# M2 of the large blocks as products of 12-bit parts, with the units of weights' parts and the fourth block's first steps at other places

## The chip, the cores and the metric

The kernel runs on one core of a Trainium2 chip. The engines work side by side, each on its own queue in program order: TensorE (PE; PEld is its weight load), VectorE (DVE), ScalarE (ACT), GpSimd (POOL), and SyncE (SP), which here issues the DMAs. The metric is the device time of one execution in microseconds (us). All times inside the kernel are counted from the start of its span.

## The reference

A retention layer for 4 x 8 heads over 768 positions of width 64, whose output, as 3072 tokens x 512, goes through a layer with ELU:

```python
for t in range(S):
    state = gamma[None, :, None, None] * state + np.einsum('bhd,bhe->bhde', k[:, :, t], v[:, :, t])
    y[:, :, t] = scale * np.einsum('bhd,bhde->bhe', q[:, :, t], state)
...
h = x @ w_in
g = np.where(h > 0.0, h, alpha * (np.exp(np.minimum(h, 0.0)) - 1.0))
return (g @ w_out).astype(np.float32)
```

`w_in` is 512 x 2048 and `w_out` 2048 x 512, all in float32.

## The kernel before

**Token blocks.** The 3072 tokens are six blocks of 512 (tb 0 to 5). Blocks 0 and 1 go through the two layers by themselves; blocks 2 and 3, and then 4 and 5, go together as "large blocks" (nb 0 and 1 in the loop `for nb in range(NB)`). Retention is done in chunks of 128 tokens (`scores`, `states`, `outputs`: 64 x 64 products), and each step of it is set by hand between the products of the layers: `retention_step(tb, step)`.

**Products.** The layers use a seven-product scheme (products 1 to 7, or M1 to M7 for a large block). A float32 matmul of TensorE is two records in the trace. In a large block's first layer, M2, M1, M3 and M7 are each split again into seven products (`big_twice`, products at L1268, two calls with `at` 0 and 1 for each M; `ORDER1`), and so M2 too is done "by two levels". M6 and M4 are done another way (`passes`, L1330): weights and inputs are cut into parts of 12 bits, so that a product of two parts is exact in one pass over the rows. With `hi` and `lo` parts of the weights, and a third plane that serves the correction (`d`), a 128-row tile takes six matmuls of 512 columns: four with `hi` and `lo`, two with `d`. The results are put together by `stt(..., 4097.0, ...)`, which is one VectorE instruction. M5 is plain float32 (`big_rest`, L1317). Then `second_big` (L1376) is the second layer. For blocks 0 and 1 the first layer of block 1 is `first` / `strassen` (L784) and the second layer `second_twice` (L977).

**Parts of weights.** A unit (n, j) is a quarter of layer j's weights. `parts_of_layer` (L919) takes a tile, makes `hi` on ScalarE (L923), `lo` on VectorE (L917) and `d` on GpSimd (L925), and gives back two sends of 512 KB and 256 KB, which go to DRAM (`scratch5`). The sends are issued by SyncE in program order and wait there for the tile's VectorE and GpSimd instructions. `next_part` (L1701) issues the sends of the unit before and begins the next one. The list `units` has eight; six are made during the first layer of block 1 (rounds n = 0 to 3 of the loop at L1706: two in round 1, three in round 2, one in round 3), in two tiles of the pool `wide`, and two in `side` of the first large block, in the tile of the pool `x6`. A tile is written again when both sends of the unit that had it have landed.

**A round.** In a round, products 1 and 2 of round n are issued, between them and after them products 3 and 4 of round n - 1, and then 6, 7 and 5. ScalarE copies results out of the PSUM banks: `kept` (L726, after products 6 and 5), and `nc.scalar.copy(pb, pa)` (L743), which must be done before product 2 adds onto bank pb. Places in a round at which a unit can be begun: after product 2, then `at` 0, 1 and 2, after products 6, 7 and 5. In round 3, retention of block 2 starts: four masks (L342), four scalings of v on VectorE (`scale_v`, L305).

**Weights from DRAM.** After round 3 the ring of slots opens: eight tiles of 256 KB and, while block 1's second layer runs, three more. `want(...)` lists the pieces in the order of their use; `fetch` (L854) issues a load whenever a slot is free, and `done` gives a slot back behind the product that read it. All loads of weights, the chunks of q, k, v (1 MB each, `load`, L125), the sends (`send_small`, L679) and the stores of the output share SyncE's queue. In the first large block, products 1, 2 and 4 of `big_twice` read their weights from `w_all`, so that M2 loads 1 MB; in the second one, 1.75 MB. The sums of M2's weights are made by `combine_small(2)` and sent beside the first layer of block 1, and `send_quarters(2)` sends the rest. `big_x(j)` makes M_j's inputs, four VectorE subtractions; `split_x` (L933) makes the three planes of an input to `passes`, one ScalarE and two VectorE instructions.

## Time and profile before

| | |
|---|---|
| median of 3 runs | 615.33 us (614.37 to 616.35) |
| the profiled execution | 612.33 us |
| its span, first to last instruction | 610.6 us |

Busy us of the engines by stage, and the mean busy share of the 16 DMA engines:

| stage (us) | what | PE | DVE | ACT | POOL | DMA share | GB/s |
|---|---|---|---|---|---|---|---|
| 133 to 183 | first layer of block 1, parts | 49.82 | 43.64 | 25.44 | 8.42 | 0.87 | 279 |
| 183 to 237 | second layer of block 1, retention | 54.00 | 47.05 | 11.07 | 3.49 | 0.91 | 318 |
| 237 to 262 | M2 of the first large block, retention of block 3 | 23.98 | 18.36 | 6.59 | 1.04 | 0.66 | 216 |
| 262 to 298 | its M1, M3, M7 | 36.00 | 33.25 | 22.43 | 3.54 | 0.95 | 293 |
| 298 to 333 | its M6, M4, M5 | 34.79 | 32.84 | 28.98 | 34.15 | 0.84 | 274 |
| 333 to 440 | its second layer, retention of blocks 4 and 5 | 107.00 | 86.61 | 17.58 | 5.60 | 0.58 | 177 |

The stages go on in the same way for the second large block. In a line of the timeline the first number is the start, the second the length of what was merged into the line; in brackets stands the idle time ahead of it and what ended it. Lengths of TensorE's lines overlap, since matmuls are pipelined; the starts tell how long something took. The chain of waits follows the end of the kernel back to what released each step.

### The profile page before, as it was taken

The numbers are of one execution on the slowest core, as the hardware profiler recorded it, in microseconds if no ns is written. First come the engines' busy times: TensorE is split into PE (matmuls) and PEld (weight loads), VectorE is DVE, ScalarE is ACT, GpSimd is POOL, SyncE is SP. The second block draws the span as 40 slices with busy tenths as digits, with TensorE's granted clock in tenths as the row PEclk, the third lists the DMA queues.
The fourth block names the chain that finished last, engine by engine and source line by source line (L and its number), as shares of the span: only waits on it lengthen the run. The fifth ranks groups of instructions, "written<-read, shape, count | busy, mean of one in ns | idle before, by whom it ended". The sixth has DMA issues, their size and how long they took to land.

```text
span 610.6 us, 13767 instructions
## 1 busy us (share of the span) xinstructions
PE 602.7 (99%) x5510; PEld 492.5 (81%) x5510; DVE 506.5 (83%) x778; ACT 262.3 (43%) x448; POOL 97.0 (16%) x75
## 2 busy tenths in 40 slices
PE   8999999999999999999999999999999999999997
PEld 6765568888889998888766888888888866788886
DVE  5769889989799886889998787898658999778785
ACT  6899744205553112147689310100236778611110
POOL 2011000000220001000697000110000398000000
PEclk9999999999999999999999999999999999999999
DMA  8698569789977999599986455874554676656553
GB/s 318 272 389 308 172 215 270 234 244 259 353 236 242 296 394 325 182 299 258 307 286 222 125 136 156 271 272 115 191 166 154 172 206 191 166 152 188 152 151 116
DMA packets 87856, 139.85 MB, mean 229 GB/s; under 512 B 7024, under 2 KB 48752, under 8 KB 83056
## 3 DMA queue, kind: packets, MB, share of 16 engines
q1 hardware_dynamic: 87792, 138.96, 71.3%
q8 instruction: 44, 0.72, 0.5%
q14 instruction: 20, 0.16, 0.1%
HBM read 105.12 MB, written 33.82 MB: 228 GB/s over the span
## 4 chain that ended last, share of the span: by engine, by line
PE 92%; DMA 3%; DVE 2%; POOL 1%; issue 0%; ACT 0%; ACTq 0%; DVEq 0%
PE pa L1376 16%; PE pa L1268 8%; PE pd L1376 8%; PE pa L977 4%; PE pb L1376 4%; PE pd L1268 4%; PE pa L557 3%; PE x L647 3%; PE pa L784 3%; PE x L1330 3%; PE pa L647 2%; PE pa L1317 2%; PE pb L1268 2%; PE sc L331 2%; PE pd L977 2%; PE kv L371 2%
## 5 line engine op out<-in xcount | busy, mean ns | idle before, releaser
L1384 ACT COPY ms<-pa 128x256 f32<-128x256 f32 x41 | 15.2, 372 | 107.5 <-PE pa L1376 103.0
L1376 PE MATMUL pa<-gC,wq 128*128 128x256 f32 x240 | 56.8, 382 | 0.0
L1376 PEld LDWEIGHTS pa<-gC,wq 128*128 128x128 f32 x240 | 45.1, 190 | 7.2 <-issue 1.0
L305 POOL TENSOR_TENSOR chunk<-chunk,vf 128x512 f32<-128x512 f32 x15 | 19.1, 1278 | 164.9 <-DMA chunk<-in_qkv_dram 120.2
L1343 ACT ACTIVATE r<-r 128x512 f32<-128x512 f32 x64 | 40.4, 631 | 2.0
L1279 ACT COPY m<-pa 128x512 f32<-128x512 f32 x32 | 18.7, 584 | 38.5 <-PE pa L1268 35.1
L1388 DVE TENSOR_TENSOR res<-pd,ms 128x256 f32<-128x256 f32 x26 | 11.0, 422 | 28.2 <-PE pd L1376 17.4
L1376 PE MATMUL pd<-w_all,wq 128*128 128x256 f32 x120 | 28.3, 379 | 0.0
L1344 DVE SCALAR_TENSOR_TENSOR gC<-r,gC 128x512 f32<-128x512 f32 x24 | 27.6, 1158 | 0.0
L925 POOL TENSOR_TENSOR wp<-wp 128x512 fp32r<-128x512 f32 x6 | 8.4, 1404 | 116.3 <-DMA scratch_dram<-wi 102.8
L1376 PEld LDWEIGHTS pd<-w_all,wq 128*128 128x128 f32 x120 | 22.8, 190 | 3.1
L1833 POOL TENSOR_TENSOR chunk<-chunk,w_all 128x512 f32<-128x512 f32 x4 | 5.1, 1298 | 127.1 <-DVE gC L1348 127.1
L183 ACT ACTIVATE w_all<-wraw 128x1024 uint32<-128x1024 uint32 (+1 forms) x19 | 19.1, 1007 | 14.0 <-PE x L647 9.8
L1358 DVE TENSOR_TENSOR gC<-w_all,gC 128x1024 f32<-128x1024 f32 x20 | 24.2, 1260 | 0.0
L1376 PE MATMUL pa<-ts,wq 128*128 128x256 f32 x96 | 22.9, 381 | 0.0
L1376 PE MATMUL pa<-w_all,wq 128*128 128x256 f32 x96 | 22.9, 381 | 0.0
L185 ACT ACTIVATE w_all<-wraw 128x1024 fp8e4<-128x1024 f32 (+1 forms) x19 | 22.6, 1190 | 0.6
L1376 PE MATMUL pd<-ts,wq 128*128 128x256 f32 x96 | 22.7, 379 | 0.0
L557 PE MATMUL pa<-xb,w_all 128*128 128x512 f32 x48 | 21.5, 597 | 0.0
L1410 ACT COPY res<-pa 128x256 f32<-128x256 f32 x13 | 4.8, 372 | 38.1 <-PE pa L1376 38.1
L213 DVE CUSTOM_DVE_ANT_0 w_all<-wraw,w_all 128x2048 uint16<-128x2048 uint16 (+1 forms) x19 | 20.1, 1057 | 0.8
L514 ACT ACTIVATE r<-r 128x512 f32<-128x512 f32 x32 | 20.2, 630 | 1.0
(361 smaller groups left out, 1606.7 us busy)
## 6 DMA issues: line engine op xcount, KB each, us to landing
wq<-scratch_dram SPq DMA_DIRECT2D x231, 256.0 KB, 3.5
chunk<-in_qkv_dram SPq DMA_DIRECT2D x22, 1024.0 KB, 7.3
wraw<-in_w_dram SPq DMA_DIRECT2D x15, 1024.0 KB, 6.1
scratch_dram<-wp SPq DMA_DIRECT2D x8, 512.0 KB, 4.0
out_dram<-res SPq DMA_DIRECT2D x7, 512.0 KB, 3.4
scratch_dram<-gT SPq DMA_DIRECT2D x12, 256.0 KB, 4.3
wq<-scratch_dram SPq DMA_DIRECT2D x24, 128.0 KB, 3.2
scratch_dram<-w_all SPq DMA_DIRECT2D x24, 128.0 KB, 3.0
```

The costliest lines, as they stand in the source:

```text
L183: nc.scalar.activation(flat, lo, AF.Copy, scale=2.0**-29)
L185: nc.scalar.activation(top, hi.bitcast(FP32), AF.Copy, scale=2.0**-120, saturate=False)
L213: vec.tensor_tensor(out=flat, in0=c, in1=flat, op=ALU.add)
L514: nc.scalar.activation(e, e, AF.Exp, scale=-1.0)
L557: nc.tensor.matmul(hp, lhsT=w[n][:, fi, j // 2, j % 2, :], rhs=xb[:, j, :], start=(j == 0), stop=(j == 3))
L647: nc.tensor.matmul(X[j][:, d, :], lhsT=w[j][:, d * P : d * P + P], rhs=x[j], start=(n == 0 and d == 0), stop=at_end, skip_group_check=True,)
L977: nc.tensor.matmul(ps, lhsT=w[:, f, :], rhs=ts[j][k][:, f, :], start=(begin and f == 0), stop=(f == 3), skip_group_check=True,)
L1268: nc.tensor.matmul(ps[:, f, :], lhsT=w[:, f, :], rhs=big_xs[j][k], start=(begin and f == 0), stop=True, skip_group_check=True,)
L1343: nc.scalar.activation(r, r, AF.Exp, scale=-1.0)
L1344: return lambda: nc.vector.scalar_tensor_tensor(g, r, -1.0, h, ALU.add, ALU.max)
L1358: nc.vector.tensor_tensor(out=quarter(to, r, t), in0=quarter(x, r, t), in1=quarter(y, r, t), op=op)
L1376: nc.tensor.matmul(ps, lhsT=w[:, f, :], rhs=ts[j][k][:, f // 2, f % 2, :], start=(begin and f == 0), stop=(f == 3), skip_group_check=True,)
```

## The change

- M2 of a large block is done by `one_layer`: for each of eight tiles four matmuls with `hi` and `lo` and two with `d`, one ScalarE copy and one VectorE `stt`. Its input is split by `split_x` into planes: `hi` and `lo` in the tile of `x6`, the third in the pool `top`. `combine_small(2)`, `send_quarters(2)` and `big_x(2)` go.
- Layer 2 joins `LAYER`, and its four units join the list, which now has twelve. They go to `scratch6`, and M2 wants twelve pieces of 256 KB from there.
- The first unit is made in round 0, in a tile of the pool `stage`; three follow in round 1 (after products 2, 7 and 5), four in round 2 (after 2, 6, 7 and 5), two in round 3 (after 2 and 7), all of these in the two `wide` tiles. The last two are made in `side`, at places (2, 2) and (3, 2), where before they stood at (0, 2) and (1, 2).
- `scores(3, 0)` is issued at the end of step 4 of block 1's second layer, and `states(3, 0)` at the end of step 5; the later steps of block 3's retention come a place sooner in the first large block, but for its last, which comes at `at` 2.

```diff
-    W_IN = {1: w_a_[:, :, :, 0], 2: w_a_[:, :, :, 1], 3: w_x_[:, :, :, 1], 7: w_x_[:, :, :, 0]}
-    AMONG = {2: 0, 3: 1, 7: 2, 1: 3}
+    W_IN = {1: w_a_[:, :, :, 0], 3: w_x_[:, :, :, 1], 7: w_x_[:, :, :, 0]}
+    AMONG = {3: 0, 7: 1, 1: 2}
...
-    LAYER = {4: w_b_[:, :, :, 1], 5: w_b_[:, :, :, 0], 6: w_y_}
+    LAYER = {2: w_a_[:, :, :, 1], 4: w_b_[:, :, :, 1], 5: w_b_[:, :, :, 0], 6: w_y_}
...
-        to = scratch5[2 * n : 2 * n + 2].rearrange("f q p c -> q p f c")
-        c = 0 if j == 6 else TH
+        if j == 2:
+            to = scratch6[2 * n : 2 * n + 2].rearrange("f p c -> p f c")
+            third = scratch6[2 * NQ + n].rearrange("p (f c) -> p f c", f=2)
...
     def open_x():
...
+        t = shared["x6"].tile([P, 2, 2, TB], F32R, name="xr", tag="x")
+        return t, open_top([P, 2, 2, TB], F32R)[:, 0]
...
+        for m, i in (("K", 0), ("D", 0), ("K", 1), ("D", 1), ("K", 2), ("K", 3), ("D", 2), ("K", 4), ("K", 5), ("D", 3), ("K", 6), ("K", 7)):
+            want((tb, m, i), scratch6[i + (2 * NQ if m == "D" else 0)])
+        for j, at in ORDER1[2:]:
...
+    def one_layer(n, at):
+
+        tb, banks = n + 2, {}
+
+        def product(m, third):
+            name = (tb, "D", m // 2) if third else (tb, "K", m)
+            ps = bank("bd"[m % 2] if third else "a")
+            todo = [(planes[2][2], m % 2 * TH)] if third else [(planes[2][0], 0), (planes[2][1], TH)]
+            for x, c in todo:
+                for k in range(2):
+                    nc.tensor.matmul(
+                        joined(ps), lhsT=where[name][:, c + k * P : c + k * P + P].bitcast(F32R), rhs=x[:, k],
+                        start=(k == 0 and x is todo[0][0]), stop=(k == 1), skip_group_check=True,
+                    )
+            banks[m, third] = ps
+            if m % 2 or not third:
+                done(name)
+
+        for m in range(4 * at, 4 * at + 4):
+            for third in (True, False) if m else (False, True):
+                product(m, third)
+            if m % 4 == 0:
+                yield
+            nc.scalar.copy(tile_of("C11", m), banks[m, True])
+            stt(tile_of("C11", m), banks[m, False], 4097.0, tile_of("C11", m), ALU.add)
+            if m % 4 in (1, 2):
+                yield
...
-    units, made = [(0, 6), (0, 4), (1, 6), (1, 4), (2, 6), (3, 6), (2, 4), (3, 4)], []
-
-    def next_part(make=True):
+    units, made = [], []
+    units += [(0, 2), (1, 2), (0, 6), (0, 4), (1, 6), (2, 2), (1, 4), (2, 6), (3, 2), (3, 6), (2, 4), (3, 4)]
+
+    def next_part(make=True, pool=None):
         to_send.extend(made)
         send_small()
-        made[:] = parts_of_layer(wide.tile([P, 2, 3, TH], F32R, name="wp", tag="wp"), *units.pop(0)) if make else []
+        made.clear()
+        if make:
+            t = (pool or wide).tile([P, 2, 3, TH], F32R, name="wp", tag="stage" if pool else "wp")
+            made[:] = parts_of_layer(t, *units.pop(0))
...
-        if n > 1:
+        if n:
             next_part()
...
-            if n and at:
-                next_part(n < 3)
+            if n == 2 or n and at:
+                next_part(n < 3 or at < 2)
             if at == 1 and n == 0:
-                some(smalls[2], 2)
+                next_part(True, stage)
...
     def next_block():
-        open_x()
-        run(big_x(2))
+        t, d = open_x()
+        planes[2] = [t[:, 0], t[:, 1], d]
+        split[:] = [split_x(planes[2], xa[:, 2:4])]
+        some(split[0], 2)
...
+        if at == (4, "end"):
+            scores(3, 0)
+        elif at == (5, "end"):
+            states(3, 0)
         if s == ORDER2[-1]:
             break
-    scores(3, 0)
+    run(split[0])
...
-            if units and (at, place) in ((0, 2), (1, 2)):
+            if units and (at, place) in ((2, 2), (3, 2)):
...
-            1: lambda: (send_quarters(2), send_layer(5, range(NQ))), 2: lambda: send_quarters(3),
+            1: lambda: send_layer(5, range(NQ)), 2: lambda: send_quarters(3),
...
-            cur = big_twice(nb, j, sub)
+            cur = one_layer(nb, sub) if j == 2 else big_twice(nb, j, sub)
+            if at == 1:
+                run(tail)
             next(cur)
+            if at == 2:
+                open_quarters()
...
+            if at == 2 and nb == 0:
+                retention_step(3, 4)
...
-            if at == 1 and nb == 0:
-                retention_step(3, 2)
...
             if nb == 0:
                 if at == 0:
-                    states(3, 0)
+                    scores(3, 1)
                 elif at == 1:
-                    retention_step(3, 3)
+                    retention_step(3, 2)
...
                 if at == 0:
-                    scores(3, 1)
                     states(3, 1)
                 elif at == 1:
-                    retention_step(3, 4)
-                    run(tail)
+                    retention_step(3, 3)
```

## The prediction

> **What bounds the kernel now.** I read the page first, then TensorE's timeline around M2, then the queues of ScalarE and SyncE where the parts of weights are made.
>
> ```profile
> PE 602.7 (99%) x5510; PEld 492.5 (81%) x5510; DVE 506.5 (83%) x778; ACT 262.3 (43%) x448; POOL 97.0 (16%) x75
> ```
>
> TensorE is busy 602.7 of 610.6 us at the full granted clock. Time is won only by giving it less to do, and whatever makes it wait is paid in full. The two kinds of product (timeline of TensorE: start, length, line):
>
> ```profile
> 310.95 0.63 PE L1330 MATMUL x<-xl,wq 128*128 128x512 f32 x2
> 311.42 1.09 PE L1330 MATMUL pa<-xr,wq 128*128 128x512 f32 x4
> 312.35 1.88 PE L1317 MATMUL pa<-xb,w_all 128*128 128x512 f32 x4
> ...
> 445.19 1.03 PE L1268 MATMUL pa<-xt,wq 128*128 128x256 f32 x4
> ...
> 451.31 1.03 PE L1268 MATMUL pa<-xt,wq 128*128 128x256 f32 x4
> ```
>
> Lengths overlap, so starts count. Six products of parts (L1330) go from 310.95 to 312.35: 0.233 us each. One half of an M by two levels (L1268; seven rows, 445.19 to 451.31) is 6.12 us.
>
> Where parts are made, ScalarE's timeline shows a wait that TensorE feels:
>
> ```profile
> 163.76 0.57 ACT L726 COPY m<-pa 128x512 f32<-128x512 f32 x1
> 167.13 0.63 ACT L923 ACTIVATE wp<-w_all 128x512 fp32r<-128x512 f32 x1 [2.80 <-DMA scratch_dram<-wp]
> 167.67 0.57 ACT L726 COPY m<-pa 128x512 f32<-128x512 f32 x1
> 169.09 0.63 ACT L923 ACTIVATE wp<-w_all 128x512 fp32r<-128x512 f32 x1 [0.86 <-DMA scratch_dram<-wp]
> 169.63 0.58 ACT L743 COPY pb<-pa 128x512 f32<-128x512 f32 x1
> ```
>
> There are two `wide` tiles, so a unit cannot begin until the store of the unit two before it has landed. Behind it in ScalarE's queue stand the copies that free TensorE's banks. TensorE just got by:
>
> ```profile
> 168.29 1.99 PE L784 MATMUL pa<-xt,w_all 128*128 128x256 f32 x8 [0.18 <-ACT m L726]
> 170.26 1.99 PE L784 MATMUL pb<-xt,w_all 128*128 128x256 f32 x8
> ...
> 183.33 1.16 PE L977 MATMUL pa<-gC,wq 128*128 128x128 f32 x8
> ```
>
> SyncE's queue explains the wait (an entry spans several issues, with the waits between them):
>
> ```profile
> 156.13 0.94 SPq L125 DMA_DIRECT2D chunk<-in_qkv_dram  x2
> 157.16 19.55 SPq L679 DMA_DIRECT2D scratch_dram<-wp  x10
> 176.76 20.59 SPq L854 DMA_DIRECT2D wq<-scratch_dram  x20
> ```
>
> Two loads of 1 MB go ahead of a unit's store, and the chain of waits gives that store this line:
>
> ```profile
> 157.94 9.08 DMA scratch_dram<-wp
> ```
>
> **M2 itself: -2.2 us.** Per block two halves of 6.12 (12.24) become 8 tiles x 6 products x 0.233 = 11.18: -1.06, twice -2.1; I write -2.2 with the switches of shape between halves. Bounds: 0 (rival 4) to -3.2 (with the 1.0 us that TensorE idled at 244 and 249, between the retention products that move). Per tile ScalarE copies once (0.58) and VectorE adds once (0.70), under 1.40 us of TensorE; if that cover went, a bank would be late by the excess alone.
>
> **A. Ten units instead of six in the first layer of the second 512 tokens: +3.4 us.** Unit 1 has a tile of its own; units 2 to 10 share two. Round 1 now makes units 2, 3, 4 and round 2 makes 5, 6, 7, 8. Unit 4 stands where the second unit stood (ScalarE at 154.73, GpSimd done at 157.9); its store still follows the two loads, so it lands at 167.0, and unit 6 starts at 167.1, as in the row. A unit begun there had GpSimd's part done at 169.85, and its 256 KB store took 2.5 us: 172.4. Only then can unit 8 begin, which stands just ahead of the copy to pb; before, that place was reached at 169.09. From there to TensorE's next product took 1.17 us (170.26 - 169.09): 172.45 + 1.17 = 173.6, 3.4 late. Unit 7's wait (store of unit 5, 163.3 + 5.7 = 169.0, then the copy, so L784 at 170.3 for 168.29) lies inside it. Bounds: +0.4 with 2.5 us for unit 4's store too; +6.6 if unit 4 lands 1 us later (more is queued) and unit 6 takes the 4.7 us that the next store took. The first end needs an empty DMA queue, but the DMA share is 0.9 to 1.08 from 148 to 168; I keep the row's value.
> [...]
>
> **B. The ring's first load is late: +3.7 us.** Before, the last sends of parts were through at 176.7 and SyncE went on to the second layer's weights (L854), the first of which took 4.1 us: at hand at 180.9, needed at 183.33. Unit 10 is now made one step later, behind product 7 of round 3. On TensorE's own clock, shifts aside: VectorE is full from 177.39 with four masks (2.41), then this line, of which the first of four stands ahead of the unit:
>
> ```profile
> 179.79 2.48 DVE L305 TENSOR_TENSOR chunk<-chunk,vf 128x512 f32<-128x512 f32 x4
> ```
>
> So unit 10's VectorE part ends at 180.4 + 0.7 = 181.1 and GpSimd's (1.28) at 182.4. Its sends hold SyncE until then, and all ring loads stand behind them: first issue 182.9, landed 187.0, needed at 183.33. Bounds: 1.7 (shortest landing of such a load, 2.1) to 6.2 (6.6, as loads issued at 183 took). Later pieces are no longer late: two further steps of 1.73 us lie between the second and third.
>
> **C. M2's weights in the third block's turn: +1.8 us.** Before, three of seven products read `w_all`, and M2 loaded 1 MB; now 12 pieces of 256 KB, one per 0.93 us, right after a stage in which the DMA is full:
>
> ```profile
> 233.67 0.45 SPq L125 DMA_DIRECT2D chunk<-in_qkv_dram  x1
> 234.22 0.40 SPq L854 DMA_DIRECT2D wq<-scratch_dram  x1
> ...
> 238.41 4.70 SPq L854 DMA_DIRECT2D wq<-scratch_dram  x5
> ```
>
> The piece issued at 234.22 took 8.3 us, to 242.5. In the new order it is the third (K1), wanted 1.9 us after M2 starts at about 236: 4.5 us of waiting at the worst. Against this, the scores and states that move into steps 4 and 5 load no weights and drain about 1 us of backlog, and between 250 and 256 the DMA was idle. Bounds 0 to +4.5; between far ends I take 1.8, nearer the low one, since retention products and the 8 slots can stretch over it. In the fourth turn the DMA share before M2 is 0.51 and the pieces come early: 0.
>
> **The rest: 0.** `scores(3, 0)` and `states(3, 0)` issue no DMA; their chunks were loaded at 197.7 and 209.6 and scaled on GpSimd well before the step, and SyncE is not held by them. They cost TensorE about 1 us each at either place. VectorE loses four subtractions of 0.68 and gains four of 0.69. `split_x` costs ScalarE 1.06 and VectorE 2 x 1.22, for 4 x 0.42 gone; it starts some 4 us ahead of M2, and uncovered it is 0.8 a block. Units 11 and 12 move two M's on (2.8 us of VectorE, where it works 33.25 of 36 us): 0 to +1.5. The waits of their sends hold the ring's loads as they did before, two M's earlier.
>
> Sum: -2.2 + 3.4 + 3.7 + 1.8 = **+6.7 us**; profiled execution 612.33 (span 610.6) to 619.0. The shown median is 615.33, 3.0 above that execution: **622.0**.
>
> **Rivals.** 0.3% (1.85 us) is about what this kernel's measurement tells from no change.
> 1. *The stores land as in an empty queue (other side: not slower).* The eight 128 KB sends of M2's sums leave round 1, which speaks for it; that three units take their place, against. Then A is 0.4, B 1.7, C 0: -2.2 + 2.1 = -0.1, 615.2; if the idle 1.0 and the step before pb are won too, 613. It decides when unit 4's store lands before 163.8, where unit 6 could start. Chance 0.19, 0.11 of it under 613.5. [...]
> 2. *Only one of A and B shows.* The late ring hides behind something that I missed, or A does: +3, 618.3. For it: 1.73 us steps of cover nearby. Against: both waits stand in in-order queues. 0.17.
> 3. *DMA-bound through.* The 2.1 MB of added traffic keeps every landing at 8 us: A 6.6, B 6.2, C 4.5, late units 1, less 2.2: +16, 631. Against: the share falls to 0.38 at 168. 0.08.
> 4. *Products of parts are no cheaper*: at 12.24 / 48 = 0.255 us the gain is gone: 624. The rows show 0.233; 0.03.
> My forecast has 0.53, its own range 618 to 626.
>
> Faster: 0.11. Same: 0.08 of rival 1 and 0.02 of rival 2: 0.10. Slower 0.79. The range 614 to 628 leaves out most of the 0.11 and of rival 3.
>
> **What would show it.** M2's tiles at 1.40 us each (gain). A: L923 waiting some 3 us for `scratch_dram<-wp` three times in round 2, the last ahead of L743, and TensorE idle before pb's L784. B: the first L854 issue about 6 us nearer to the first L977, which waits for `wq`. C: idle of TensorE at the new parts' line on DMA. I am wrong if L923's waits are under 1 us, or if the first L977 follows on without idle time.

## The result, and the profile after

The changed kernel takes 640.61 us (median of 4 runs, 639.33 to 643.36), the kernel before, run beside it, 614.85 us (613.14 to 616.35): 1.0426 times as long, with a 95% interval of 1.0382 to 1.047. The profiled execution took 639.33 us, its span is 637.4 us, 26.8 us more than before. The forecast was 622.0 us: slower was right, the size was not, and neither was the range.

Of the page of the changed kernel, the busy times, TensorE's clock and the chain of waits by engine:

```profile
PE 608.5 (95%) x5494; PEld 492.4 (77%) x5494; DVE 513.7 (81%) x778; ACT 265.9 (42%) x454; POOL 102.4 (16%) x79
...
PEclk9999999999999999897999999999999999999999
...
PE 80%; DMA 8%; DVE 6%; POOL 2%; issue 2%; ACT 1%; SPq 0%; ACTq 0%; DVEq 0%; POOLq 0%
```

TensorE has less to do (16 instructions fewer) and shows 5.8 us more of busy time. Both cannot come from the work, so some of it ran slowly: PEclk, nines all through before, has an 8 and a 7 here, near 255 and 290 us. The mean granted clock is 0.989 where it was 1.000; 0.011 of 637.4 us is 7.0 us. Some 0.9 of it fell into idle time (1.7 us of idle time at half clock between 292.63 and 296.43), where a low clock costs nothing. So about 6 us is an estimate of what the clock alone took. The rest is idle time, and the chain, 92% TensorE before, is 80% now.

Where TensorE waited (its list of waits: what it was about to write and the line, what ended the wait, then us in total, times, the longest):

```profile
PE pa L1276 <- ACT m L1287: 5.5, 1, 5.5
PE pa L1327 <- DMA wq<-scratch_dram: 3.5, 1, 3.5
PE pb L785 <- ACT pb L744: 3.0, 2, 1.7
PE pa L980 <- DMA wq<-scratch_dram: 2.6, 3, 1.8
PE pb L1327 <- DVE xr L916: 2.2, 1, 2.2
```

These five make 16.8 us, two shorter ones for VectorE (1.3 at L1276, 1.0 at L372) another 2.3, and no wait of before is among them. L785 is the first layer, L980 the second layer of block 1, L1327 the new M2 (`one_layer`), L1276 the products of M1, M3 and M7. The largest, 5.5 us, is in a place to which the prediction's sum had given nothing.

Stage lengths in us, by the starts of the same products in each trace. "First layer" runs from its first product on to product 2 of round 3 (the one that waits for the copy to pb), "to layer 2" from there to the first product of block 1's second layer; "layer 2" is cut at the third product behind that one. "M2" ends at M1's second product, "M1, M3, M7" at the first product of M6, and "M2 to M7" is the stretch from M2's first product to M6's first in the second large block (the expectations call it "M2 of the second large block", but M1, M3 and M7 are in it). The last column is the clock of the profiled execution:

| kernel | first layer | to layer 2 | layer 2 | M2 | M1, M3, M7 | M2 to M7, second large block | span | clock |
|---|---|---|---|---|---|---|---|---|
| before | 36.9 | 13.1 | 1.9 + 51.7 | 23.0 | 35.2 | 51.6 | 610.6 | 1.000 |
| changed | 41.3 | 16.2 | 3.5 + 55.7 | 25.3 | 44.9 | 53.6 | 637.4 | 0.989 |
| e1_x6 | 42.5 | 17.0 | 3.6 + 54.5 | 22.4 | 37.4 | 55.5 | 632.2 | 0.992 |
| e7_before_x6 | 37.2 | 13.1 | 1.9 + 52.6 | 23.5 | 49.0 | 51.9 | 628.6 | 0.989 |
| e2_five | 36.4 | 17.3 | 3.6 + 55.3 | 26.4 | 45.1 | 55.8 | 639.8 | 0.979 |
| e5_ring | 36.4 | 16.1 | 1.9 + 54.0 | 26.4 | 44.8 | 55.6 | 636.3 | 0.988 |
| e4_load | 41.5 | 16.1 | 4.4 + 54.7 | 21.6 | 46.5 | 55.6 | 638.1 | 0.984 |
| e3_third | 41.4 | 16.0 | 4.5 + 55.1 | 26.3 | 45.3 | 51.8 | 637.2 | 0.980 |
| e8_fill | 41.8 | 16.2 | 4.3 + 56.9 | 23.6 | 45.7 | 55.6 | 642.1 | 0.984 |
| e9_three | 36.4 | 13.9 | 1.9 + 55.1 | 26.4 | 43.1 | 51.7 | 625.4 | 0.992 |
| e11_four | 37.6 | 13.0 | 1.9 + 54.1 | 22.6 | 37.6 | 51.5 | 615.1 | 1.000 |
| e12_pool | 37.6 | 13.0 | 1.9 + 56.8 | 20.5 | 38.1 | 51.1 | 616.5 | 1.000 |
| e13_split | 37.6 | 13.0 | 1.9 + 55.3 | 20.8 | 39.4 | 51.1 | 616.6 | 0.999 |
| e14_late | 37.6 | 13.0 | 1.9 + 56.8 | 20.1 | 37.3 | 52.0 | 615.7 | 1.000 |

With the change 1.1 us of `states(3, 0)` go from M2's stage to the second layer's. The stages that are not shown differ by at most 2 us. In the changed kernel the stages shown lost 4.3, 3.2, 5.6, 2.4, 9.7 and 2.1 us; the first layer began 0.6 us sooner. The ratios below leave out executions more than 1.5% above the fastest of the same kernel: two of e2's, one each of e11's and e12's.

Three places on ScalarE's queue of the changed kernel (start, length, line; the idle time ahead and what ended it):

```profile
157.23 0.63 ACT L922 ACTIVATE wp<-w_all 128x512 fp32r<-128x512 f32 x1 [2.87 <-DMA scratch_dram<-wp]
...
172.87 0.63 ACT L922 ACTIVATE wp<-w_all 128x512 fp32r<-128x512 f32 x1 [2.63 <-POOL wp L924]
173.41 0.58 ACT L744 COPY pb<-pa 128x512 f32<-128x512 f32 x1
...
292.23 0.63 ACT L922 ACTIVATE wp<-w_all 128x512 fp32r<-128x512 f32 x1 [7.23 <-DMA scratch_dram<-wp]
292.76 0.57 ACT L1287 COPY m<-pa 128x512 f32<-128x512 f32 x1
```

The second and third lines are what the prediction called A: unit 8's step, late, and behind it the copy to pb at 173.41 that TensorE waits for (before: 169.63). Unit 8 needs unit 6's tile, whose `d` was done at 170.27. The idle time is put down to GpSimd's step of unit 7, which ended at 172.77; the chain of waits names the store of unit 6's `d`, which ended at the same moment:

```profile
170.30 2.46 DMA scratch_dram<-wp
```

The first line is one more wait of the same kind, which the prediction did not have: unit 4 waits for unit 2's store, ahead of the copy to pb of round 2, and TensorE stood 1.21 us there. The last pair is the same thing again at a place where nobody had looked. Unit 12 can be written into the one tile of `x6` only when unit 11's store has landed; ScalarE stood 7.23 us, and behind it stood the lift of a bank. SyncE's queue says why the store was late (an entry spans several issues):

```profile
158.61 28.36 SPq L680 DMA_DIRECT2D scratch_dram<-wp  x14
187.02 18.86 SPq L855 DMA_DIRECT2D wq<-scratch_dram  x20
...
279.06 5.28 SPq L680 DMA_DIRECT2D scratch_dram<-wi  x8
284.38 3.13 SPq L680 DMA_DIRECT2D scratch_dram<-w_all  x6
287.61 0.43 SPq L855 DMA_DIRECT2D wq<-scratch_dram  x1
288.14 0.91 SPq L680 DMA_DIRECT2D scratch_dram<-wp  x2
```

VectorE had unit 11 ready at 280.7 (in the large blocks it makes `d` too). Its two sends come last in a queue of fourteen other sends and a load, and are issued at 288.14; the data lands at 292.1. The first two lines are B: the sends of parts hold the queue until 187.0 (before: 176.8), and the second layer's first load with them. In the chain of waits, unit 10's `d` is done on GpSimd at 186.59 and that load, issued at 187.02, lands at 190.23.

TensorE's own queue in the large blocks:

```profile
254.97 1.94 PE L1327 MATMUL pa<-xr,wq 128*128 128x512 f32 x4 [3.50 <-DMA wq<-scratch_dram]
256.84 1.89 PE L332 MATMUL sc<-chunk 64*64 64x64 f32 x64
...
259.23 1.09 PE L1327 MATMUL pa<-xr,wq 128*128 128x512 f32 x4
...
293.38 2.07 PE L1276 MATMUL pa<-xr,wq 128*128 128x256 f32 x4 [5.47 <-ACT m L1287]
296.43 2.07 PE L1276 MATMUL pd<-xr,wq 128*128 128x256 f32 x4 [0.98 <-DVE chunk L1291]
...
469.92 0.62 PE L1327 MATMUL pb<-xr,wq 128*128 128x512 f32 x2
...
471.29 0.61 PE L1327 MATMUL pd<-xr,wq 128*128 128x512 f32 x2
```

Two things are to be read here. The last two rows, one M2 tile apart, start 1.37 us one after the other, the next tile at 472.64 after 1.35, those before after 1.46 and 1.39: the forecast was 1.40. So the work itself became cheaper, by about 1 us a block. And four matmuls that take 1.09 us at 259.23 take 1.94 us right behind the wait of 3.50. The windows of the same kernel give the granted clock there (us; busy time and instructions of PE, PEld, DVE, ACT and POOL; clock; DMA share; GB/s):

```profile
255.00:257.00 2.00, 2.00 (x8) 1.16 (x12) 0.00 (x0) 0.00 (x0) 0.00 (x0) 0.52 0.85 271
...
259.00:261.00 2.00, 2.00 (x54) 1.50 (x56) 1.65 (x3) 0.59 (x1) 0.00 (x0) 1.00 0.89 306
```

Half clock behind a wait, then full clock again; from 293 to 299 us it is 0.50. Of the 9.7 us that M1, M3 and M7 lost, 5.47 + 0.98 are idle time; of the 3.25 left over, some 2.5 are these slow rows, by the starts of the same rows in e1, and 0.29 is a third idle time.

### The profile page after: what moved, and what is told of

Same layout as the page of the kernel before. It is cut to its first block, busy times and chain, and to the rows that moved or that the text cites. A ratio compares the mean times of both kernels' runs of the same rounds, so it can differ in the third digit from the quotient of the medians.

```text
span 637.4 us, 13780 instructions
## 1 busy us (share of the span) xinstructions
PE 608.5 (95%) x5494; PEld 492.4 (77%) x5494; DVE 513.7 (81%) x778; ACT 265.9 (42%) x454; POOL 102.4 (16%) x79
## 2 busy tenths in 40 slices
DMA packets 88687, 144.55 MB, mean 227 GB/s; under 512 B 7088, under 2 KB 46512, under 8 KB 83888
## 4 chain that ended last, share of the span: by engine, by line
PE 80%; DMA 8%; DVE 6%; POOL 2%; issue 2%; ACT 1%; SPq 0%; ACTq 0%; DVEq 0%; POOLq 0%
PE pa L1412 15%; PE pd L1412 7%; PE pa L1276 5%; PE pb L1412 4%; DMA wq<-scratch_dram 3%; PE pa L558 3%; PE x L648 3%; DMA scratch_dram<-wp 3%; PE pd L1276 3%; PE x L1366 3%; PE pa L980 2%; PE pa L648 2%; PE pa L1353 2%; PE pa L1327 2%; PE y L428 2%; PE pb L558 2%
## 5 line engine op out<-in xcount | busy, mean ns | idle before, releaser
L1412 PE MATMUL pa<-gC,wq 128*128 128x256 f32 x240 | 56.8, 381 | 0.0
L1412 PEld LDWEIGHTS pa<-gC,wq 128*128 128x128 f32 x240 | 45.1, 190 | 7.3 <-issue 1.0
L1379 ACT ACTIVATE r<-r 128x512 f32<-128x512 f32 x64 | 40.4, 631 | 2.0
L924 POOL TENSOR_TENSOR wp<-wp 128x512 fp32r<-128x512 f32 x10 | 14.3, 1425 | 121.2 <-DVE wp L916 121.2
L1412 PE MATMUL pd<-w_all,wq 128*128 128x256 f32 x120 | 28.3, 379 | 0.0
L1380 DVE SCALAR_TENSOR_TENSOR gC<-r,gC 128x512 f32<-128x512 f32 x24 | 27.6, 1157 | 0.0
L1412 PEld LDWEIGHTS pd<-w_all,wq 128*128 128x128 f32 x120 | 22.8, 190 | 3.1
L1287 ACT COPY m<-pa 128x512 f32<-128x512 f32 x24 | 14.0, 582 | 22.1 <-PE pa L1276 19.1
L1412 PE MATMUL pa<-w_all,wq 128*128 128x256 f32 x96 | 22.9, 381 | 0.0
L1412 PE MATMUL pa<-ts,wq 128*128 128x256 f32 x96 | 22.9, 381 | 0.0
L186 ACT ACTIVATE w_all<-wraw 128x1024 fp8e4<-128x1024 f32 (+1 forms) x19 | 22.6, 1189 | 0.6
L1412 PE MATMUL pd<-ts,wq 128*128 128x256 f32 x96 | 22.7, 379 | 0.0
L1327 PE MATMUL pa<-xr,wq 128*128 128x512 f32 x64 | 18.6, 414 | 4.1 <-DMA wq<-scratch_dram 3.5
L988 ACT COPY ms<-pa 128x128 f32<-128x128 f32 x21 | 5.6, 265 | 36.9 <-PE pa L980 36.9
```

Source lines behind the costliest of these rows:

```text
L186: nc.scalar.activation(top, hi.bitcast(FP32), AF.Copy, scale=2.0**-120, saturate=False)
L1327: nc.tensor.matmul(joined(ps), lhsT=where[name][:, c + k * P : c + k * P + P].bitcast(F32R), rhs=x[:, k], start=(k == 0 and x is todo[0][0 ...
L1379: nc.scalar.activation(r, r, AF.Exp, scale=-1.0)
L1380: return lambda: nc.vector.scalar_tensor_tensor(g, r, -1.0, h, ALU.add, ALU.max)
L1412: nc.tensor.matmul(ps, lhsT=w[:, f, :], rhs=ts[j][k][:, f // 2, f % 2, :], start=(begin and f == 0), stop=(f == 3), skip_group_check=True,)
```

## The experiments

Each edit is told against the changed kernel, where nothing else is said. Ratios are to the kernel before, run beside it on the same chip.

### e1_x6: unit 11 begun one place sooner, so that its sends leave ahead of the fourteen others

Unit 11 is begun at (2, 1), sent at (2, 2); unit 12 stays at (3, 2).

```diff
-            if units and (at, place) in ((2, 2), (3, 2)):
+            if units and (at, place) in ((2, 1), (3, 2)):
-            elif made and place == 1:
+            elif made and place == (2 if at == 2 else 1):
```

> The changed kernel, with the eleventh unit of parts begun one place sooner (2, 1) and its sends issued at (2, 2), ahead of fourteen small sends. Theory (the wait of the twelfth unit for the one tile of x6 holds ScalarE and so TensorE): the idle 5.5 and 1.0 us at 288 to 297 and the half clock behind it go, some 8 to 9 us, about 631 us; the DMA bytes are the same. Rival (the DMA is too full through the kernel): less than 1.5 us is won, the wait turns up again at another place.

Measured: 631.59 us (629.26 to 633.93), ratio 1.0258 [1.0218, 1.0298], 9 us less than the changed kernel. M1, M3 and M7 took 37.4 us in place of 44.9. On TensorE the wait for ScalarE is gone, and two waits for VectorE are left, this one and one of 0.66:

```profile
281.65 1.13 PE L1276 MATMUL pd<-w_all,wq 128*128 128x256 f32 x4 [1.29 <-DVE chunk L1291]
```

The row has its full speed (1.13, where rows behind the wait took 2.07). So one place of one unit cost 7.5 us in its stage, idle time and slow clock together. M2, ahead of the edit, is 2.9 us shorter here too; its waits for weights are 0.51 and 1.45 in place of 3.50; why, the runs do not show.

### e7_before_x6: the kernel before, with nothing but the two units at the changed kernel's places

```diff
-            if units and (at, place) in ((0, 2), (1, 2)):
+            if units and (at, place) in ((2, 2), (3, 2)):
```

> The kernel before, with nothing changed but the two units made in the large block: at places (2, 2) and (3, 2) instead of (0, 2) and (1, 2). Theory (that place alone makes ScalarE wait, since fourteen small sends stand ahead of the first unit's sends): 5 to 9 us slower than before, 620 to 624, with TensorE idle about 5 us where M1 ends. Rival (it takes M2's added loads as well): within 1.5 us of before.

Measured: 627.66 us (626.2 to 630.38), ratio 1.0212 [1.017, 1.0254]: 12 us for this one line alone, more than the 5 to 9 of the theory, without new products, units or traffic. The stage went from 35.2 to 49.0 us, and TensorE has the row of the changed kernel, only longer:

```profile
285.07 2.07 PE L1268 MATMUL pa<-tq,wq 128*128 128x256 f32 x4 [9.00 <-ACT m L1279]
```

Together with the last run this shows the cause both ways: taken out of the changed kernel the wait goes, put into the kernel before it comes.

### e2_five: five tiles for the units of the first layer

Units 4, 5 and 6 go into the three tiles of the pool `stage`, so that none waits for a store in round 2.

```diff
+        pool = stage if 12 - len(units) in (0, 3, 4, 5) else None
```

> The changed kernel, with units 4, 5 and 6 in the three tiles of the pool stage, so that five tiles serve instead of two; the same bytes at the same places in SyncE's queue. Theory (two tiles make ScalarE wait for stores): product 2 of round 3 starts at about 170 instead of 174.0 us, 4 us are won there, the late ring load stays (VectorE and GpSimd of unit 10 are no sooner on TensorE's clock). Rival (the stores are late because the DMA is full, and TensorE waits for them in any case): under 1 us is won.

Measured: 643.12 us (633.45 to 645.59), ratio 1.0367 [1.0278, 1.0456]. The four runs lie 12 us apart, so the total says nothing. The stage does: the first layer took 36.4 us (before 36.9, changed 41.3), without idle time in its rounds. A is ScalarE's wait for a tile. But the time did not reach the end: 1.1 us was lost at once to VectorE's `scale_v` (2.26 us of waiting, 1.02 in the changed kernel), TensorE still waited 1.47 us for the ring's first load (B), and M2 to M7 of the second large block took 55.8 in place of 53.6 us, at a mean clock of 0.979 over the whole.

### e5_ring: as the last, and units 9 and 10 begun one place sooner

Unit 10's sends then leave SyncE before the second layer needs its weights.

```diff
+        if n == 3:
+            next_part()
...
-                next_part(n < 3 or at < 2)
+                next_part(n < 3) if n < 3 or at < 2 else None
```

> As the one with five tiles, and unit 10 made right behind unit 9, its sends one place sooner. Theory (the ring's first load stands behind unit 10's sends in SyncE's queue): the first second-layer product (183.33 us before the change, 190.3 with it) follows on without idle time, at 182 to 184; 8 to 9 us in all are won against the changed kernel, 631 to 632. Rival (the first load is late since the DMA is full): it still comes 3 us or more late.

Measured: 636.25 us (633.03 to 638.03), ratio 1.0341 [1.0298, 1.0384]. The second layer's first product no longer waits for `wq`, and the 1.9 us to its third product (3.5 in the changed kernel) show the full clock there. Yet "to layer 2" is still 16.1 us: a unit's steps on VectorE, begun sooner, hold up two other things, 1.21 us for `h` at 178.65 and 1.19 for `chunk` at 183.63. B's wait was taken away and two new ones came in its stage; M2's wait for its weights grew from 3.50 to 4.64 us.

### e4_load: two loads of 1 MB one step sooner

They stand ahead of the fetches of M2's first pieces in SyncE's queue and on the DMA engines.

```diff
-    LOADS = {(1, "first"): 0, (2, "end"): 1, (4, "end"): 2, (5, "end"): 3}
+    LOADS = {(1, "first"): 0, (2, "end"): 1, (3, "end"): 2, (4, "end"): 3}
```

> The changed kernel, with the last two chunk loads of 1 MB one step sooner, so that none stands ahead of M2's first pieces in SyncE's queue. Theory (the third piece, K1, is late because 1 MB goes ahead of it): the idle 3.5 us in M2 of the first large block falls under 1.5 us, M2's stage from 25.3 to 22 or 23 us. Rival (the DMA is full over the whole second layer, and it matters little in which order): the wait only moves, over 2.5 us of idle stay in M2 or as much turns up sooner, in the second layer (55.7 us).

Measured: 639.57 us (637.47 to 641.97), ratio 1.0393 [1.0362, 1.0425]. M2 of the first large block took 21.6 us, less than before (23.0), with this in the place of the 3.50:

```profile
252.91 1.17 PE L1327 MATMUL pa<-xr,wq 128*128 128x512 f32 x4 [0.49 <-DMA wq<-scratch_dram]
```

C is the order of the loads, then, and 3.7 us of the stage hang on it. (Of the 23.0, 1.1 are the states that moved, so that 21.6 is a little over the 20.8 due with M2's gain.) In the total 1 us of it is seen: M1, M3 and M7 took 46.5 us (44.9), and M2 to M7 of the second large block 55.6 (53.6). TensorE's waits there are the same, 5.55 and 2.23 us (5.47 and 2.23); but the clock was half from 289.61 to 299.85 us, 10.2 us (6.8 in the changed kernel), and fell behind the 2.23 too, where the changed kernel's trace has it at 1.00.

### e3_third: the third plane of the second large block's input made at once

In the changed kernel VectorE makes it behind the retention's last outputs, 2.2 us too late for M2.

```diff
-        some(split[0], 2)
+        run(split[0])
...
-    run(split[0])
...
-        if more:
-            run(split[0])
```

> The changed kernel, with the third plane of M2's input made right behind the other two, ahead of the retention outputs, not behind them. Theory (in the fourth turn the first product with that plane waits for VectorE, which is at the outputs): the idle 2.2 us ahead of it goes, 2 to 3 us are won in the stage M2 of the second large block (53.6 us in the changed kernel, 51 to 52 expected; 2 more where the clock would have fallen after the idle time). Rival (VectorE is only busy by chance there, the plane is late in any case): the idle stays over 1 us.

Measured: 638.73 us (636.24 to 639.3), ratio 1.037 [1.0345, 1.0396]. The wait is gone and M2 to M7 of the second large block take 51.8 us, 1.8 less; 0.52 us of waiting for `res` stays there.

### e8_fill: four products more in the wait

Four products whose result nobody reads, into a spare bank, go behind the first tile of M2 in the first large block, to keep TensorE busy while it waits for weights. They take 3.45 us and are no part of the work.

```diff
+            if n == 0 and m == 0:
+                for _ in range(4):
+                    nc.tensor.matmul(spare, lhsT=xa[:, 2, 0:P], rhs=xa[:, 3, :], start=True, stop=True, ...)
```

> The changed kernel, with four extra float32 products of 128x512 whose result nobody reads between M2's first tile and its second in the first large block, 3.45 us of TensorE in the place where it waits for the piece K1. Theory (after some 3 us of idle time TensorE's clock is halved for a while): the four matmuls behind the wait take 0.93 us and not 1.94, the scores behind them 1.0 and not 1.8, and M2's stage is 1.5 to 2 us shorter than 25.3 although more is done. Rival (the clock falls for another reason, or the long rows are the records'): the stage takes 25.3 us or more.

Measured: 642.09 us (640.14 to 643.87), ratio 1.0432 [1.0405, 1.0459]. On TensorE, the rows that were slow behind the wait:

```profile
258.42 1.09 PE L1327 MATMUL pa<-xr,wq 128*128 128x512 f32 x4
259.44 1.16 PE L332 MATMUL sc<-chunk 64*64 64x64 f32 x64
```

The four matmuls start 1.02 us ahead of the next row (1.87 us in the changed kernel) and the scores take 1.16 (1.89); the clock in 255 to 260 us is 1.00. M2's stage, with 3.45 us more to do, took 1.8 us less. So here the waiting itself, not what was waited for, made the rows slow. The total did not fall: elsewhere the clock was low for longer than in the changed kernel, 0.85 in 195 to 205 us, 0.81 in 300 to 310 and 0.74 in 465 to 470.

### e9_three: five tiles, the third plane at once, one unit less in round 3 and three in the large block

```diff
+        pool = stage if 12 - len(units) in (0, 3, 4, 5) else None
...
-            if units and (at, place) in ((2, 2), (3, 2)):
+            if units and (at, place) in ((2, 1), (3, 1), (4, 1)):
-            elif made and place == 1:
+            elif made and place == 2:
...
```

Unit 10, made in the large block here, is made from weights that have been overwritten by then; the work is the same.

> Five tiles, the third plane early, and three units (not two) in the large block, at (2, 1), (3, 1) and (4, 1), their sends one place later each; round 3 of the first layer makes one unit, as before the change. Theory (the loss is in the waits, one by one): first layer and first ring load as before the change (36.9 + 15.0 us from the first layer's start to the last product 3 of it), M1 to M7 35 to 38 us, M2 of the second large block 50.5 to 52; what stays is the third-turn M2 (3 us) and the second layer (2 us): 616 to 621 us. Rival (2.1 MB of added traffic cost their time whatever the order): over 626 us.

Measured: 625.62 us (623.78 to 627.28), ratio 1.0155 [1.0132, 1.0178]. Without unit 10 in round 3, and with the tiles, A is gone and B but for 0.8 us (36.4, 13.9 and 1.9 us; before 36.9, 13.1 and 1.9). Three units in `x6` are one too many: M1, M3 and M7 took 43.1 us with four waits of 0.73 to 2.55. The time lies above the 616 to 621 of the theory and just under the rival's 626.

### e11_four: all cures at once, two units in `x6`

Five tiles (units 1, 4, 5, 6 and 9); four units in round 1, four in round 2, one in round 3; `x6` as in e1, the loads as in e4, the third plane as in e3. Nothing is left out.

```diff
+        pool = stage if 12 - len(units) in (0, 3, 4, 5, 8) else None
...
-            if n == 2 or n and at:
-                next_part(n < 3 or at < 2)
+            if n in (1, 2) or n == 3 and at == 1:
+                next_part(n < 3)
...
```

> All cures at once, on the changed kernel: five tiles for the units made in the first layer, one unit less in round 3 of it, unit 11 sent one pass later and unit 12 sent a pass later (so that each has the spare tile landed and sent with time to spare), the third plane of the second large block split at once, the chunk loads behind which the second layer's matrices stand moved one step sooner. No work is left out. Theory (the losses are separate waits, each in a place of its own, and the half clock comes only behind them): first layer 36.5 + 13.9 to 15.0 us where the changed kernel has 41.3 + 16.2; M2 of the first large block 21.6; M1 to M7 36 to 37.5; M2 of the second 51.6; the second layer 53 to 55; 614 to 618 us in all, within 0.5% of the kernel before, clock 0.995 or more. Rival (the DMA queues carry too much, so that a wait taken away comes back in the next stage): one or two of these stages stay 3 us or more above the figure, and the time is 624 or more.

Measured: 618.46 us (616.25 to 626.07, 12 runs; before 613.30), ratio 1.0058 [1.0032, 1.0085], clock 1.000. The changed kernel had stood 25.8 us above the kernel before beside it, this one stands 5.2 above: 20.6 us are back. Measured in the same way, e1 had brought 9.7 us, e5 (with e2's tiles) 5.1, e3 2.0 and e4 1.2, 18 in all; e2's runs lie too far apart to say. The rival, in which a full DMA gives every wait back one stage on, had 624 or more. It is a little slower than the kernel before all the same. Against it: +0.6 us up to the second layer, +2.1 in the second layer and M2 together (76.75 for 74.65), +2.3 in M1, M3 and M7 (1.29 and 0.66 us for VectorE's additions), 0.0 in M2 to M7 of the second large block, where M2's gain of 1.06 was due.

### e12_pool: units 11 and 12 with GpSimd making `d`

```diff
-                made[:] = parts_of_layer(t, *units.pop(0), nc.vector)
+                made[:] = parts_of_layer(t, *units.pop(0))
```

(against e11_four)

> As the run with all cures, but the low parts of units 11 and 12 are made on GpSimd and no longer on VectorE, between M1 and M7 of the first large block. Theory: the two idle times of 1.29 and 0.66 us for VectorE's additions, which were left in those places when only the two units were moved, go, since 0.7 us of VectorE's queue a unit is taken away ahead of them: M1 to M7 35 to 36 us and 1 to 2 us less in all than the run with all cures. Rival (VectorE is late by its own additions, whatever the units do): both idle times stay, and the time is the same within 0.5 us; or GpSimd is slower by a multiple, the unit's send comes later, and ScalarE waits for the tile again: 1 us or more above it.

Measured: 618.98 us (616.15 to 626.52, 12 runs), ratio 1.0077 [1.005, 1.0105]: no better. The two waits for VectorE grew, to 1.64 and 1.01 us. VectorE's queue shows that work taken off it came back as slower work:

```profile
268.46 1.49 DVE L947 TENSOR_TENSOR xr<-xb,xr 128x256 f32<-128x256 f32 x1
...
276.64 2.30 DVE L1384 TENSOR_TENSOR gC<-gC,chunk 128x1024 f32<-128x1024 f32 x1
```

The same two lines take 0.42 and 1.22 us in e11_four. Each met one of GpSimd's two additions (from 268.07 and from 276.47) and took 1.07 to 1.08 us longer, against 0.69 saved.

### e13_split and e14_late: other places for the steps of units 11 and 12

e13_split issues ScalarE's step of unit 11 at (2, 0) and VectorE's at (2, 1), and all of unit 12 at (3, 1); in e14_late unit 12 has ScalarE's step at (3, 2) and VectorE's at (4, 0).

```diff
-            if units and (at, place) in ((2, 1), (3, 2)):
+            if units and (at, place) in ((2, 0), (3, 1)):
...
-                made[:] = parts_of_layer(t, *units.pop(0), nc.vector)
+                half[:] = [t, *units.pop(0), nc.vector]
+                parts_of_layer(*half, step=0)
+            if half and (at, place) in ((2, 1), (3, 1)):
+                made[:] = parts_of_layer(*half, step=1)
+                half.clear()
```

> As the run with all cures, but the steps of units 11 and 12 stand elsewhere in the queues: ScalarE's step of unit 11 is issued a third of a product earlier than VectorE's two, so that VectorE does not stand 1.07 us behind it (265.93 us in that run, behind ScalarE's step of 265.27), and all three steps of unit 12 one third of a product earlier, where VectorE was idle for 0.95 us (before 273.44). No work is added or left out. Theory (the 1.29 and 0.66 us in which TensorE waits for VectorE's additions there are order, not load): both idle times go to 0.3 us or less each, M1 to M7 of the first large block 35.5 to 36.2 us in place of 37.55, and the whole 1 to 2 us below the run with all cures: 0.3 to 0.5% above the kernel before. Rival (VectorE is simply full there): M1 to M7 stays at 37 us or more and the whole time within 0.5 us of that run.

Measured for e13_split: 618.75 us (617.94 to 621.26), ratio 1.009 [1.006, 1.0119]. Unit 11's wait of 1.29 us is gone, as the theory had it. Unit 12 went wrong: at its new place unit 11's store, 6.7 us under way, had not landed, and ScalarE's queue has the old picture again:

```profile
273.65 0.63 ACT L923 ACTIVATE wp<-w_all 128x512 fp32r<-128x512 f32 x1 [2.52 <-DMA scratch_dram<-wp]
```

TensorE waited 2.57 us behind it, and 1.06 us for VectorE after that; M1, M3 and M7 took 39.4 us.

> As the run before it, but unit 12 is made later in place of sooner: ScalarE's step where it stood in the run with all cures (there at 273.12 us, behind the landing of unit 11's store, which the last run had at 273.5), VectorE's two steps one third of a product behind it. Unit 11 as in the last run. Theory (a place for a unit must lie behind the landing of the store before it and where VectorE has room; both can be had): no idle time of over 0.7 us in M1 to M7 of the first large block, the stage 35.3 to 36.5 us, M2 20.7, the whole 616 to 617.5 us, 0.3 to 0.5% above the kernel before. Rival (the time that these steps take from VectorE is lost wherever they stand): M1 to M7 37 us or more, and 618 us or more.

Measured for e14_late: 617.59 us (616.26 to 621.5), ratio 1.0086 [1.0055, 1.0117]. Unit 12's step waited 1.16 us for unit 11's store, and TensorE did not feel it. M1, M3 and M7 took 37.3 us, with one wait of 1.52 us left (at 285.53) for a lift that stood in ScalarE's queue behind `split_x`. That one makes M6's input in the same tile of `x6`, and waited for unit 12's store:

```profile
283.94 1.06 ACT L941 ACTIVATE xr<-xr 128x1024 fp32r<-128x1024 f32 x1 [3.77 <-DMA scratch_dram<-wp]
```

The rival's 37 us came true, by another way than it said: TensorE waited for ScalarE behind a late store, not for VectorE. M2 took 20.1 us, 2.5 less than in e11_four, but the second layer took 2.6 more, with idle times of 1.21 and 1.22 us. In all four of the last kernels the two stages together take 76.0 to 77.3 us, however the waits are spread over them.

## Why the prediction was wrong

**The step that failed** stands under "The rest: 0": "Units 11 and 12 move two M's on (...): 0 to +1.5. The waits of their sends hold the ring's loads as they did before, two M's earlier." It priced the move by VectorE's room, and by what the sends hold up. It did not ask what holds up the sends. At the new place fourteen sends of 128 KB stand ahead of unit 11's in SyncE's queue, and unit 12 wants the same single tile one M later. That stage lost 9.7 us in the changed kernel; e7 lost 12 us by the places alone, and e1 won 9 back. The term stood at nothing in the sum and at 1.5 at most. All that was needed stood in the profile: the chain "tile free when the store has landed, lift behind it in ScalarE's queue" is A's own, and it was not carried to the other pool.

**A second omission:** the half clock was not priced anywhere. Every wait was costed at its length; in the changed kernel's trace the rows took twice as long for 3.41 us at a time behind the waits of 1.80 and 3.50, for 6.83 behind the 5.47. This is about 6 of the 26.8 us.

**The same paragraph** held `split_x` to be covered, "uncovered it is 0.8 a block". In the first large block that was right. In the second the third plane came behind the retention in VectorE's queue: 2.23 us of waiting, and 1.8 back in e3. The cover was looked at in one block of two.

**M2 itself, -2.2:** right, about -1.06 a block (tiles of 1.35 to 1.46 us). e13 shows what is left of it in M2 to M7 of the second large block: 51.1 us for 51.6, with 0.52 of a wait for `res` in it.

**A, +3.4:** right in mechanism and near in size, 4.34. One part was missed: unit 4 was taken to begin at 154.73, and began at 157.23, behind unit 2's store (1.21 us of TensorE). Its own store landed at 167.09 all the same (forecast 167.0). The marks were there: ScalarE waits three times in round 2 (1.28, 1.32 and 2.63 us, where some 3 each was forecast), the last ahead of the copy to pb, and unit 8 begins at 172.87 (forecast 172.45). e2 shows it with tiles alone.

**B, +3.7:** right in mechanism; 3.16 up to the first product and 1.59 behind it, the latter half clock. The first load landed 3.25 us after its issue, where 4.1 was taken. Of the 3.16, TensorE spent 1.02 waiting for VectorE's scaling of v and then 1.80 for the load. The first was not in the prediction: unit 10's step stands behind the first of the four scalings, and the other three took 2.96 us, where all four had taken 2.48. The lateness was near in size, its echo was missed. What cures it is not only a sooner place (e5), but a unit less in round 3 (e9, e11).

**C, +1.8 of 0 to 4.5:** the wait was 3.50 us, in the range but nearer its far end, and it came where it was said. The claim that the backlog drains under scores and states did not hold: in the 11.4 us ahead of M2 the DMA share is 1.00, and K1 took 9.25 us from issue to landing, where the piece it was priced by had taken 8.3. Nor was the DMA idle between 250 and 256 us before the change, as the prediction read it: it was so to 253 us, and then busy at 0.87 to 1.08. The second layer itself, which had no term, lost 2.9 us besides the moved states.

**The rivals.** Rival 3, DMA-bound through, gave 631 us and came nearest to the total, but for the wrong reason: e11 moves the same bytes and is at 1.0058. What the DMA may still take are some 3 us in the second layer and M2 (76 to 77.3 us, where 74.65 less the gain of 1.06 was due). The page counts 144.55 MB for 139.85, 4.7 more, where the prediction had 2.1; between 200 and 260 us e11 moved 19.0 MB and the kernel before 17.9 (rates of the windows times their lengths), and 1.1 MB at the 367 GB/s that the kernel before moved from 220 to 240 us are 3.0 us. That fits, but no run took bytes away, so it is argued, not shown.

**Single cures** mostly add up: 18 us of the 20.6 that e11 brings, which also makes a unit less in round 3. That a total falls less than its stage goes, in the traces, with the clock. What is missing of a mean clock of 1, times the span, is 7.0 us in the changed kernel's trace, 13.4 in e2's, 12.7 in e3's, 10.2 in e4's and 10.3 in e8's.

**Open:** the some 3 us in the second layer and M2, and why M2's waits were shorter in e1. No version beat the kernel before: the 2.1 us that the two blocks win did not pay, in any order tried, for four units more.

## What to carry to other kernels

When a step that writes a shared tile is moved, follow its tile round: who writes it last, where that writer's store stands in the issuing queue at the new place, and what is queued behind the waiting instruction; do so for each pool, not only for the one that looked tight. Price a wait of TensorE above its length: behind waits of 1.80, 3.50 and 5.47 us the changed kernel's clock was half for 3.41, 3.41 and 6.83 us. And judge a cure by the stage it is meant for as well as by the total: in e4 1 of the 3.7 us that M2's stage won was seen in the total, with the clock half for 10.2 us in a later stage in place of 6.8.

## What was not expected of the hardware

**The clock halved behind short waits.** 0.50 to 0.52 behind 3.50 and 5.47 us of idle time, rows twice as long (1.94 for 1.09 us; 2.07 for 1.13); also behind 1.80 us at 190.27, where a wait of 1.02 us had gone before, three us earlier. With TensorE kept busy by products that nobody reads the clock was 1.00 from 255 to 260 us (e8). But in e11 idle times of 1.13 and 0.95 us, 3 us apart, left it at 1.00.

**The same wait cost the clock in some traces and not in others.** The changed kernel's clock falls at 190.23, 255.08 and 292.63 us and is full again from 193.64, 258.50 and 299.46. From each of these six to the next are 3.41, 61.44, 3.42, 34.13 and 6.83 us: 1, 18, 1, 10 and 2 times 3.413 (109.23 us from the first to the last, over 32). In e4 the 10.24 us from 289.61 to 299.85 are 3 times that. Cut into stretches of 3.413 us by these marks, from 130 to 605 us, the changed kernel's trace shows this: the clock fell behind the three stretches in which TensorE was busy for 0.00, 0.03 and 0.35 of the time, and behind no other (the next lowest, from 169.75 us, has 0.58); it came back behind stretches busy for 0.99, 1.00 and 0.89, and stayed half behind one of 0.61. The wait of 2.23 us lies across two of them (0.63 and 0.72) in that trace, and the eight matmuls of L1412 behind it, at 461.42, took 1.89 us. In e4 the same wait lies inside one stretch (456.86 to 460.28 by its own marks, busy 0.35), and the eight took 3.48 us; in e8 they took 3.53. M2 to M7 of the second large block took 55.6 us in both and 55.5 to 55.8 in e1, e2 and e5, which have that wait too, where the changed kernel took 53.6.

**Some of VectorE's additions took longer while GpSimd added:** 1.49 us for 0.42 and 2.30 for 1.22 in e12, both with two operands in SBUF. Both began after one of GpSimd's additions had begun, and ended after it had ended (269.95 and 278.94 us, GpSimd's 269.67 and 277.86); an addition in SBUF that had begun ahead of GpSimd's (L880, at 267.85) kept its 0.68. In M6, where GpSimd adds all through, rows with an operand in PSUM kept 0.68 to 0.70 (L916, from 302.71 on), while one from SBUF beside them took 1.66 (L1380, at 303.32); in the changed kernel's M6 the two lines show 0.70 (at 321.04) and 1.70 us (at 321.65).
